# Paired-chunk loads, gated prefetch and a searched order in a sliding-window attention and two-MLP kernel

## The chip, the cores and the metric

One core of one Trainium2 chip runs the whole program. The metric is the device time of one execution in microseconds; of several runs the median is given.

## The reference

The inputs are queries, keys and values of 4 batches, 8 heads, 576 positions and 64 dimensions, and the weights of two MLPs. Everything is float32.

```python
scores = scale * q @ k.T                                  # per batch and head
scores = where(0 <= i - j < 128, scores - slope[h] * (i - j), -1e9)
attn = softmax(scores)                                    # + 1e-9 in the denominator
x = (attn @ v), heads side by side                        # 2304 tokens x 512
h = x @ w_in                                              # 2304 x 2048
x = (max(h, 0) + alpha * min(h, 0)) @ w_out               # 2304 x 512
h = max(x @ w1, x @ w2, x @ w3)                           # 2304 x 768
out = h @ w_out2                                          # 2304 x 512
```

The weights of both MLPs come as 64-bit floats, which the kernel turns into float32 itself.

## The kernel before, in words

The 2304 tokens are cut into nine chunks of 256 (c = 0 to 8). Attention works on one chunk and one pair of heads (hp = 0 to 3) at a time, so there are 36 such pairs of heads. `pair` (L710) does one: it loads queries and keys (L723), one transfer for each of the two heads, each into 64 partitions; it loads the values (L727, L751), scales the queries on POOL (L730), computes the scores on PE (L743), the softmax on DVE (L772), ACT (L778, L783) and POOL (L790), transposes on PE (L800) with copies on ACT (L808), the product with the values on PE (L820, L837, L844), and writes the result in two parts as input of the first MLP (L867 on ACT, L869 on DVE). In the first four chunks (`EARLY`) the loaded queries and keys lie in four buffers `w24` to `w27` that later hold weights; from the fifth chunk on they lie in a ring of two.

The first MLP runs through "items": a block of 128 hidden features for a chunk or two. An item's first product is L903 to L905 (`hidden_of`), the activation is L909 and L912 on DVE and L882 and L883 on ACT and DVE (tile `g`), and the second product is L931 (`products_of`). Each weight block is loaded as 64-bit words (`to_f32`, L411, tiles `w_b`, 512 KB each: `w0_b` is the first block of w_in, `w1_b` the first of w_out, and so on), split into words and rebuilt on ACT (L412, L414), DVE (L416 to L422) and POOL (L425), and split once more into two parts (`split`, L432 on ACT, L434 on DVE or POOL). A weight load is told to wait for the ACT instruction L414 of the weight four blocks earlier. Chunks 0 to 3 and all 32 weight blocks are worked on in the first 140 us. Beside and behind them come the rest of the first MLP (`pair_mlp`) and the second MLP (`second_mlp`: 18 steps of products L1057 and output products L1077, whose weights come back from DRAM by the loads at L1012).

No engine's order is written by hand. Every operation is recorded with an engine, a cost and a due time (`Plan.add`); `Plan.run` walks through all of them with these costs, and `Plan.issue` repeats that eight times (`ROUNDS`), each time with due times made from the walk before, and keeps the order whose planned end is earliest. The instructions are then put out in that order, engine by engine, and each engine executes its own in order, SP's transfers included.

Two kinds of matmuls have no use but to keep PE going: `keep_busy` in the attention of the first chunk (L366), and those that `Plan.keep_busy` puts in at L372 where PE's plan has room between 12 and 130 us:

```python
for _ in range(round((until - max(free, at) - FILL_LESS) / FILL_ONE)):
    self.idle(new())
```

Of the kernel before, what the change touches and what calls it, by code (L numbers as in the profile page):

```python
# [21 lines left out]
P = 128  # L22
# [64 lines left out]
class Plan:  # L87
# [90 lines left out]
    def issue(self):  # L178
        due, best = {op: op.due for op in self.ops}, None
        for _ in range(ROUNDS):  # L180
            start, end = self.run(due)
            whole = max(end.values())
            if not best or whole < best[0]:
                best = whole, start
            late = self.run({op: -t for op, t in end.items()}, back=True)[1]
            due = {op: -t for op, t in late.items()}

            users = {}
            for op in self.ops:
                for d in op.deps:  # L190
                    if d.eng == "sp":
                        users[d] = min(users.get(d, due[op]), due[op])
            due.update((d, t - DMA_LEAD) for d, t in users.items())
# [77 lines left out]


FILL_FROM, FILL_TO, FILL_LESS, FILL_ONE = 12.0, 130.0, 0.3, 0.215

KEEP = 3
ROUNDS = 8
DMA_LEAD = 3.0
# [13 lines left out]
def attention_then_two_mlps(ctx: ExitStack, tc: tile.TileContext, qkv, v, w_in, w_out, alpha, w123, w_out2, out):  # L291
# [59 lines left out]

    cq = const.tile([P, H // 2], F32, name="cq")
    for h in range(H):
# [52 lines left out]
    def to_f32(src, raw, wt, due, after, n=512):  # L406
# [3 lines left out]

        add("sp", 1.4 * n / 512, due - 24, lambda: nc.sync.dma_start(out=raw(), in_=src.bitcast(I32)), w=[raw], after=after)  # L411
        add("act", 0.05 + n / 966, due - 10, lambda: nc.scalar.activation(  # L412
# [294 lines left out]

    X, loads = {}, []

    def pair(k, j, hp, due):  # L710


        c = GROUPS[k][j]
        vv, z = v_r.new(), z_r.new()
        if c < EARLY:
            raw, pt = (w_s.new(2 * NF - 8 + 4 * i + (c * KD + hp) % 4, 2 + i) for i in range(2))
            ps = [p_r.new() for _ in range(2)]
        else:
            raw, pt, ps = qkv_r.new(), pt_r.new(), [p_r.new() for _ in range(2)]
        qs, heads = slice(N + P, 2 * N + P), range(2)  # L720
        for a in heads:
            rows = slice(a * D, (a + 1) * D)
            load = add("sp", 0.6, due - 16, lambda a=a, rows=rows: nc.sync.dma_start(  # L723
                out=raw()[rows, :10 * D], in_=qkv[2 * hp + a, c, rows, :10 * D]), w=[raw])
        if c == 0:
            loads.append(load)
        add("sp", 0.7, due - 9, lambda: nc.sync.dma_start(  # L727
            out=vv(), in_=v[hp, c].rearrange("p (k a d) -> p k a d", k=3, a=2)), w=[vv])

        add("pool", 0.45, due - 13, lambda: nc.gpsimd.tensor_scalar(  # L730
            out=raw()[:, qs], in0=raw()[:, qs], scalar1=cq[:, hp:hp + 1], scalar2=1.0, op0=ALU.mult, op1=ALU.mult),
            r=[raw], w=[raw])

        s = [early.new(1 + (2 * hp + a) % 3) if c == 0 else s_b.new() for a in heads]


        def scores():

            for n in range(2):
                for u in range(2):  # L740
                    for a in heads:
                        rows, b = slice(a * D, (a + 1) * D), 2 * u + n
                        nc.tensor.matmul(s[a]()[u * D:(u + 1) * D, n * R:(n + 1) * R],  # L743
                                         raw()[rows, qs.start + b * D:qs.start + (b + 1) * D],
                                         raw()[rows, b * D:b * D + R], start=True, stop=True)

        scored = yield dict(cost=0.9, due=due - 12, fn=scores, r=[raw], w=s)
        ve = ve_r.new() if c in MERGED else None
        if ve:
            for n in range(2):  # L750
                add("sp", 0.3, due - 9, lambda n=n: nc.sync.dma_start(  # L751
                    out=ve()[n * D:(n + 1) * D], in_=v[hp, c, (1 - n) * D:(2 - n) * D, n * P:(n + 2) * P].rearrange(
                        "p (k a d) -> p k a d", k=2, a=2)), w=[ve])
        if c == 0:
# [50 lines left out]
        else:  # L805
            add("pe", 0.58, due - 6, lambda: [transposes(a) for a in heads], r=ps, w=psts)
        for a in heads:
# [3 lines left out]
        if ve:  # L811
# [11 lines left out]

            at_q, handed = 2 * R, dict(cost=0.95, due=due - 3.5, fn=values, r=[pt, vv, ve])
            yield handed
            psv = handed["w"]
        else:
# [19 lines left out]

            yield dict(cost=1.1, due=due - 3.5, fn=values, r=[pt, vv, *(psv if at_q else [])], w=psv)
        if k >= PAIRED:
# [347 lines left out]
    def attend(i):  # L1197
# [3 lines left out]
        for turn, args in enumerate(list_i):  # L1201
# [7 lines left out]
            for pair_of in going[:1] if merged else list(going):  # L1209
# [8 lines left out]
                if late:  # L1218
                    first = x["fn"]
                    new.send(put(dict(cost=1.6, due=x["due"], fn=lambda first=first, scores=scores: (first(), scores["fn"]()),  # L1220
                                      r=x["r"] + scores["r"], w=x["w"])))
                else:
                    put(x)
# [81 lines left out]
```

## Time and profile before

| what | value |
| --- | --- |
| median of three runs | 787.7 us |
| the three runs | 786.4, 787.7, 790.71 us |
| the profiled execution's own time | 790.29 us |
| its span, first to last instruction | 788.4 us |
| PE busy | 767.3 us, 97% of the span |
| DVE, ACT, POOL busy | 570.6, 400.0, 359.6 us |
| mean granted clock of PE | 0.996 |

The span is what the rows of the trace are counted in, from its first instruction; the profiled execution took 1.9 us more than its span, and 2.6 us more than the median. A window gives the busy time of each engine in a stretch. A timeline row gives a start, a length, the engine, the line, the operation, the tiles (written <- read), the number of instructions, and in brackets the idle time ahead of them and what ended it. Matmul records can overlap, so the length of a group is longer than the distance to the next one.

### The profile page before, as it was taken

To read this page: it belongs to the slowest core of one execution; us is meant where nothing else is said; L and a number is where in the kernel's file an instruction comes from. 1 tells how busy PE (TensorE), PEld (TensorE's weight loads), DVE (VectorE), ACT (ScalarE), POOL (GpSimd) and SP (SyncE) were. 2 spreads that over 40 slices of the span, in tenths; PEclk is the share of its full clock that TensorE was granted. 3 is DMA by queue.
4 is the path that set the end of the run, shared out by engine and by line. 5 is a ranking of instruction groups with operands and counts; after the bars stand their busy time and mean duration, and the time that the engine had idled before them with its cause. 6 is when DMAs were issued, how large, how long until landed. Compare 5 with 4: busy or idle time off the path is not lost.

```text
span 788.4 us, 16787 instructions
## 1 busy us (share of the span) xinstructions
PE 767.3 (97%) x5881; PEld 662.5 (84%) x5887; DVE 570.6 (72%) x1382; ACT 400.0 (51%) x1113; POOL 359.6 (46%) x444
## 2 busy tenths in 40 slices
PE   7699999999999999999999999999999999999998
PEld 3478877778778788997888788899998999899996
DVE  5578898977665848999996879869983546734551
ACT  5789786756454555657674657444433102411101
POOL 5669656776655325555664432504353211702211
PEclk9989999999999999999999999999999999999999
DMA  8998355654674538356678967587795877555702
GB/s 223 246 332 269 96 167 169 203 178 146 216 254 150 178 118 298 124 168 197 206 236 255 332 197 279 204 305 261 268 357 196 271 243 252 186 188 199 227 1 80
DMA packets 85923, 167.04 MB, mean 212 GB/s; under 512 B 10576, under 2 KB 46800, under 8 KB 85840
## 3 DMA queue, kind: packets, MB, share of 16 engines
q1 hardware_dynamic: 85696, 165.98, 64.1%
q8 instruction: 46, 0.75, 0.4%
q14 instruction: 37, 0.30, 0.1%
q10 hardware_dynamic: 144, 0.01, 0.0%
HBM read 114.83 MB, written 51.12 MB: 210 GB/s over the span
## 4 chain that ended last, share of the span: by engine, by line
PE 52%; DVE 1%; ACT 0%; issue 0%; ACTq 0%
PE sb L1057 13%; PE hb L1057 12%; PE xb L615 5%; PE xb L1077 5%; PE sb L585 4%; PE hb L585 3%; PE hb L1077 3%; PE hb L615 3%; PE sb L615 3%; PE sb L1077 2%; DVE o L601 0%; DVE o L593 0%; DVE sb L593 0%; DVE g L606 0%; DVE v L419 0%
## 5 line engine op out<-in xcount | busy, mean ns | idle before, releaser
L931 PE MATMUL xb<-g,w_a 128*128 128x512 f32 (+1 forms) x624 | 127.3, 351 | 6.6 <-ACT g L882 5.8
L931 PEld LDWEIGHTS xb<-g,w_a 128*128 128x128 f32 x624 | 96.9, 191 | 24.8 <-ACT g L882 6.2
L790 POOL TENSOR_SCALAR p<-p,z 128x192 f32<-128x192 f32 x144 | 70.8, 506 | 67.7 <-DVE z L786 65.7
L425 POOL TENSOR_TENSOR v<-v,p 128x192 int32<-128x192 int32 (+1 forms) x72 | 45.8, 640 | 69.8 <-DVE v L422 23.5
L434 POOL TENSOR_TENSOR g<-p,g 128x384 fp32r<-128x384 f32 x18 | 20.9, 1161 | 116.5 <-ACT g L432 87.6
L903 PE MATMUL hb<-x_a,w_a 128*128 128x512 f32 (+1 forms) x208 | 73.2, 352 | 0.7 <-DVE x_a L869 0.7
L904 PE MATMUL hb<-x_a,w_a 128*128 128x512 f32 (+1 forms) x208 | 71.0, 341 | 0.0
L905 PE MATMUL hb<-x_a,w_a 128*128 128x512 f32 (+1 forms) x208 | 70.8, 340 | 0.0
L778 ACT ACTIVATE p<-p,z 128x192 f32<-128x192 f32 x144 | 64.4, 451 | 11.9 <-DVE z L772 11.5
L1057 PE MATMUL sb<-w_e,w_a 128*128 128x384 f32 x306 | 59.3, 334 | 0.0
L772 DVE CUSTOM_DVE_ANT_0 p<-sb,rel 128x192 f32<-128x192 f32 x128 | 39.5, 353 | 21.0 <-PE sb L743 15.1
L1057 PEld LDWEIGHTS sb<-w_e,w_a 128*128 128x128 f32 x306 | 53.8, 188 | 0.4
L425 POOL TENSOR_TENSOR wt<-wt,w_b 128x512 int32<-128x512 int32 x32 | 44.1, 1387 | 13.6 <-DVE wt L422 12.3
L615 PE MATMUL xb<-g,w_a 128*128 128x512 f32 x192 | 46.0, 389 | 0.0
L903 PEld LDWEIGHTS hb<-x_a,w_a 128*128 128x128 f32 x208 | 39.3, 189 | 7.4 <-issue 1.4
L1057 PE MATMUL hb<-w_e,x_a 128*128 128x384 f32 x234 | 45.4, 334 | 0.0
L1057 PE MATMUL hb<-w_e,w_a 128*128 128x384 f32 x234 | 45.4, 334 | 0.0
L434 POOL TENSOR_TENSOR w_a<-wt,w_a 128x512 fp32r<-128x512 f32 x25 | 34.9, 1394 | 22.2 <-ACT w_a L432 22.0
L905 PEld LDWEIGHTS hb<-x_a,w_a 128*128 128x128 f32 x208 | 39.4, 189 | 4.5
L1065 DVE TENSOR_TENSOR v<-hb,qkv 128x384 f32<-128x384 f32 x30 | 16.7, 555 | 36.6 <-PE hb L1057 36.6
L904 PEld LDWEIGHTS hb<-x_a,w_a 128*128 128x128 f32 x208 | 39.4, 189 | 4.4 <-DVE w_a L434 0.2
L432 ACT CAST w_a<-wt 128x512 fp32r<-128x512 f32 x57 | 35.0, 621 | 15.5 <-DVE wt L474 6.0
(223 smaller groups left out, 1951.0 us busy)
## 6 DMA issues: line engine op xcount, KB each, us to landing
w_a<-left SPq DMA_DIRECT2D x30, 512.0 KB, 5.2
x_a<-left SPq DMA_DIRECT2D x24, 512.0 KB, 5.3
w_b<-in_w_in SPq DMA_DIRECT2D x16, 512.0 KB, 5.7
w_b<-in_w_out SPq DMA_DIRECT2D x16, 512.0 KB, 6.2
left<-w_a SPq DMA_DIRECT2D x15, 512.0 KB, 5.6
v<-in_v SPq DMA_DIRECT2D x36, 192.0 KB, 3.2
p<-in_w SPq DMA_DIRECT2D x36, 192.0 KB, 3.2
qkv<-in_qkv SPq DMA_DIRECT2D x40, 160.0 KB, 3.0
```

The lines of the kernel that those rows point to most:

```text
L425: add("pool", n / 403, due - 5, lambda: nc.gpsimd.tensor_tensor(out=wt().bitcast(I32), in0=wt().bitcast(I32), in1=words(0), op=ALU.add), r ...
L434: add("pool" if pool_lo else "dve", n / 403 if pool_lo else 0.07 + n / 960, due + 1, lambda: eng.tensor_tensor(out=w()[:, 1, :n], in0=of() ...
L585: nc.tensor.matmul(to(), w()[:, a, ws], xs[k]()[:, b], start=(first and at_m == 0), stop=(last and at_m == 5), skip_group_check=True)
L615: nc.tensor.matmul(bs[m](), W_out[f]()[:, a, cols], g[f]()[:, b], start=(opens and f == fs[0] and not a and not b), stop=(closes and f == ...
L778: exps.append(add("act", 0.45, due - 10 + a, lambda i=i, n=n, p=p: nc.scalar.activation(out=part_of_p(p, n), in_=part_of_p(p, n), func=AF. ...
L790: z.readers.append(add("pool", 0.4, at_a + 0.2, lambda i=i, n=n, p=p: nc.gpsimd.tensor_scalar(out=part_of_p(p, n), in0=part_of_p(p, n), sc ...
L903: nc.tensor.matmul(to, wi()[:, 0, ws], x[:, 0, cols], start=(kk == 0), stop=False)
L904: nc.tensor.matmul(to, wi()[:, 1, ws], x[:, 0, cols], start=False, stop=False)
L905: nc.tensor.matmul(to, wi()[:, 0, ws], x[:, 1, cols], start=False, stop=(kk == KD - 1))
L931: nc.tensor.matmul(to, wo()[:, a, ms], g()[:, b, :n], start=(opens and not a and not b), stop=(closes and ends), skip_group_check=apart)
L1057: nc.tensor.matmul(to()[:, :TILE], Qs[q]()[:, a, ws], x[:, b], start=(first and n == 0), stop=(last and n == 5), skip_group_check=True)
L1077: nc.tensor.matmul(o(), g[j]()[:, a, b * P:(b + 1) * P], Wo[j]()[:, c], start=(j == 0 and not a and not c), stop=(j == NJ - 1 and a == 1), ...
```

## The change

Queries and keys of the first four chunks are loaded two chunks at a time: one transfer brings chunk c into partitions 0 to 63 and chunk c + 1 into partitions 64 to 127 of one buffer. For the even head of a pair of heads that is chunks 0 and 1, then 2 and 3; for the odd head chunk 0 alone (upper half, on ACT's queue), then 1 and 2, then 3 alone. The even head's data lie in `w24` to `w27`, the odd head's in `x10` to `x13`. The scale factor gets a column per head (`ch`); where only the upper half is loaded, DVE scales it, otherwise POOL. From the second chunk on every load of a pair of heads waits for the scores of the pair of heads four places back. The planner's costs for PE's attention work go up, those of some transfers go down. `Plan.issue` makes 40 trials: in each after the first the due times of the best one so far are blurred by random numbers, and four rounds start from there.

```diff
     def issue(self):
-        due, best = {op: op.due for op in self.ops}, None
-        for _ in range(ROUNDS):
-            start, end = self.run(due)
...
+        draw, best = random.Random(0), None
+        for trial in range(TRIALS):
+            if trial:
+                due = {op: t + draw.gauss(0.0, BLUR) for op, t in best[2].items()}
+            else:
+                due = {op: op.due for op in self.ops}
+            for _ in range(ROUNDS if trial else 2 * ROUNDS):
+                start, end = self.run(due)
...
+PREFETCH = 4
...
-ROUNDS = 8
+ROUNDS, TRIALS, BLUR = 4, 40, 1.5
...
-        add("sp", 1.4 * n / 512, due - 24, ...
+        add("sp", 1.35 * n / 512, due - 24, ...
...
+        qs, heads, ahead = slice(N + P, 2 * N + P), range(2), scored_ops[-PREFETCH:][:1] if c else []
         if c < EARLY:
-            raw, pt = (w_s.new(2 * NF - 8 + 4 * i + (c * KD + hp) % 4, 2 + i) for i in range(2))
+            pt, half = w_s.new(2 * NF - 4 + hp, 3), [(c + a) % 2 for a in heads]
+            for a in heads:
+                if c and half[a]:
+                    continue
+                first, last = (D if half[a] else 0), (D if c == EARLY - 1 else P)
+                KQ[hp, a] = raw = (qkv_r.new() if first == 0 and last == D else
+                                   w_s.new((2 * NF + KD * SETS[1] if a else 2 * NF - 8) + hp, 2))
+                part = slice(first, last)
+                r0 = (c - half[a]) * P + D
...
+                queue = nc.scalar if half[a] else nc.sync
+                load = add("sp", 0.82 if last - first == P else 0.6, due - 16, lambda ...:
+                           queue.dma_start(out=raw()[part, :10 * D], in_=from_[:, :10 * D]), w=[raw], after=ahead)
+                eng, e, cost = (nc.vector, "dve", 0.2) if half[a] else (nc.gpsimd, "pool", 0.45)
+                add(e, cost, due - 13, lambda ...: eng.tensor_scalar(
+                    out=raw()[part, qs], in0=raw()[part, qs], scalar1=ch[part, 2 * hp + a:2 * hp + a + 1], ...
...
-        scored = yield dict(cost=0.9, due=due - 12, fn=scores, r=[raw], w=s)
+        scored = yield dict(cost=1.0, due=due - 12, fn=scores, r=raws, w=banks)
+        scored_ops.append(scored)
```

Three places show how the order moves. The first is POOL's queue around the softmax of the fourth pair of heads (tile `z0_569`, now `z0_592`; L790, now L822, multiplies its four parts by the reciprocal sums), before and now.

```order
L730 TENSOR_SCALAR w24_c_418<-w24_c_418,cq_247 128x256
L730 TENSOR_SCALAR w25_c_452<-w25_c_452,cq_247 128x256
L790 TENSOR_SCALAR p0_568<-p0_568,z0_569 128x192
L790 TENSOR_SCALAR p0_576<-p0_576,z0_569 128x192
L790 TENSOR_SCALAR p0_568<-p0_568,z0_569 128x192
L790 TENSOR_SCALAR p0_576<-p0_576,z0_569 128x192
L425 TENSOR_TENSOR wt0_489<-wt0_489,w0_b_388 128x512
```

```order
L745 TENSOR_SCALAR x11_c_461<-x11_c_461,ch_248 128x256
L745 TENSOR_SCALAR x12_c_500<-x12_c_500,ch_248 128x256
L745 TENSOR_SCALAR x13_c_543<-x13_c_543,ch_248 128x256
L822 TENSOR_SCALAR p0_591<-p0_591,z0_592 128x192
L822 TENSOR_SCALAR p0_596<-p0_596,z0_592 128x192
L822 TENSOR_SCALAR p0_591<-p0_591,z0_592 128x192
L822 TENSOR_SCALAR p0_596<-p0_596,z0_592 128x192
L436 TENSOR_TENSOR wt0_564<-wt0_564,w1_b_412 128x512
```

The fourth pair's multiplications stood behind the scaling of the second pair of chunk 1 (`w25_c_452`); they now stand behind that of the odd heads of all four pairs of chunk 1, `x13_c_543` the last.

The second is SP's queue ahead of `w4_b`, the fifth weight block, before and now, with the semaphores that each transfer waits for (`DMAHW` is that of an earlier transfer, eight of them being used in turn; `PE`, `Pool` and `DVE` are the engines' own).

```order
L723 DMA qkv0_606<-in_qkv 64x640 [waits DMAHW5_49]
L723 DMA qkv0_606<-in_qkv 64x640 [waits DMAHW6_49]
L723 DMA qkv0_624<-in_qkv 64x640 [waits DMAHW7_49]
L723 DMA qkv0_624<-in_qkv 64x640 [waits DMAHW0_49]
L727 DMA v0_640<-in_v 128x384 [waits DMAHW1_49,PE_49]
L723 DMA w24_c_653<-in_qkv 64x640 [waits DMAHW2_49,PE_49,Pool_49]
L723 DMA w24_c_653<-in_qkv 64x640 [waits DMAHW3_49]
L411 DMA w4_b_666<-in_w_in 128x1024 [waits DMAHW4_49]
```

```order
L743 DMA x12_c_500<-in_qkv 128x640 [waits DMAHW2_49,DVE_49,PE_49]
L743 DMA x13_c_543<-in_qkv 128x640 [waits DMAHW3_49,DVE_49,PE_49]
L761 DMA v0_569<-in_v 128x384 [waits DMAHW4_49,PE_49]
L743 DMA w24_c_587<-in_qkv 128x640 [waits DMAHW5_49,PE_49,Pool_49]
L783 DMA ve0_600<-in_v 64x256 [waits DMAHW6_49]
L422 DMA w4_b_621<-in_w_in 128x1024 [waits DMAHW7_49]
L783 DMA ve0_600<-in_v 64x256 [waits DMAHW0_49]
L761 DMA v0_642<-in_v 128x384 [waits DMAHW1_49,PE_49]
L422 DMA w5_b_652<-in_w_out 128x1024 [waits DMAHW2_49]
```

The four loads of the fifth chunk (`qkv0_606`, `qkv0_624`) and one load of values are no longer ahead of `w4_b`: it was the 36th transfer of SP's queue and is now the 19th.

The third is ACT's queue around the first `g`, the activation of the MLP's first item (L882, now L914).

```order
L808 COPY w28_d_812<-sb0_781 128x384
L783 ACTIVATE z0_728<-z0_728 128x2 x2
L412 ACTIVATE wt0_817<-w4_b_666 128x512
L414 ACTIVATE w4_b_666<-w4_b_666 128x512
L412 ACTIVATE wt0_826<-w5_b_711 128x512
L882 CAST g0_844<-hb0_789 128x256
```

```order
L425 ACTIVATE w4_b_621<-w4_b_621 128x512
L840 COPY w28_d_830<-sb0_790 128x384
L840 COPY w28_d_830<-sb0_826 128x384
L914 CAST g0_834<-hb0_798 128x256
L815 ACTIVATE z0_733<-z0_733 128x2
L423 ACTIVATE wt0_853<-w4_b_621 128x512
L423 ACTIVATE wt0_857<-w5_b_652 128x512
```

Three steps on the weight blocks `w4_b` and `w5_b` stood ahead of the first `g`; one step on `w4_b` still does. Of the matmuls of the planner's own filling there were 45 and are now 28 (L372, now L383); those of the first chunk are 24 in both (L366, now L377).

## Rows read from the trace of the kernel before

**Rows 1.** The page: busy time by engine, and PE in 40 slices.
```profile
PE 767.3 (97%) x5881; PEld 662.5 (84%) x5887; DVE 570.6 (72%) x1382; ACT 400.0 (51%) x1113; POOL 359.6 (46%) x444
...
PE   7699999999999999999999999999999999999998
```

**Rows 2.** Windows: stretch, its length, then busy by engine, clock, DMA share, GB/s.
```profile
7.00:80.00 73.00, 63.28 (x800) 47.78 (x807) 50.92 (x189) 62.05 (x203) 51.36 (x73) 0.95 0.92 271
...
80.00:130.00 50.00, 49.93 (x576) 39.42 (x567) 44.30 (x120) 36.55 (x110) 31.61 (x38) 1.00 0.38 123
130.00:788.40 658.40, 652.30 (x4499) 574.36 (x4497) 473.59 (x1058) 300.12 (x800) 272.83 (x319) 1.00 0.64 212
```

**Rows 3.** Timeline of PE: start, length, work, and idle time before it.
```profile
5.17 1.56 PE L743 MATMUL xb<-w_c 64*64 64x192 f32 x16 [5.17 <-POOL w_c L730]
...
34.15 0.38 PE L372 MATMUL hb<-ident 128*128 128x512 bf16 x1
40.37 2.08 PE L931 MATMUL xb<-g,w_a 128*128 128x256 f32 x8 [5.84 <-ACT g L882]
```

**Rows 4.** Timeline of ACT, 0 to 62 us.
```profile
7.18 0.46 ACT L778 ACTIVATE p<-p,z 128x192 f32<-128x192 f32 x1 [4.76 <-DVE z L772]
...
35.93 0.66 ACT L412 ACTIVATE wt<-w_b 128x512 f32<-128x512 f32 x1 [3.19 <-DMA w_b<-in_w_in]
...
39.40 0.66 ACT L412 ACTIVATE wt<-w_b 128x512 f32<-128x512 f32 x1 [2.25 <-DMA w_b<-in_w_out]
39.96 0.36 ACT L882 CAST g<-hb 128x256 fp32r<-128x256 f32 x1
...
44.50 0.46 ACT L778 ACTIVATE p<-p,z 128x192 f32<-128x192 f32 x1 [1.21 <-DVE z L772]
```

**Rows 5.** Timeline of SP's transfers, and its waits in 10 to 60 us.
```profile
25.39 3.43 SPq L723 DMA_DIRECT2D qkv<-in_qkv  x4
28.92 0.53 SPq L727 DMA_DIRECT2D v<-in_v  x1
...
30.71 1.05 SPq L411 DMA_DIRECT2D w_b<-in_w_in  x2
...
SPq L727 <- PE hb L844: 4.3, 3, 3.5
```

**Rows 6.** Windows (columns as in rows 2): DMA at the start, stalled, and with weights.
```profile
2.00:25.00 23.00, 18.10 (x230) 10.81 (x234) 13.38 (x69) 15.93 (x63) 13.29 (x29) 1.00 1.00 240
25.00:29.00 4.00, 2.59 (x49) 1.75 (x41) 2.79 (x14) 4.00 (x16) 4.00 (x5) 1.00 0.54 148
...
41.00:45.00 4.00, 4.00 (x55) 2.97 (x54) 1.28 (x8) 2.55 (x6) 3.11 (x5) 0.60 1.03 405
```

**Rows 7.** Timeline of PE: the same five groups at two clocks end here.
```profile
45.60 0.39 PE L372 MATMUL sb<-ident 128*128 128x512 bf16 x1
...
50.61 0.88 PE L743 MATMUL sb<-w_c 64*64 64x192 f32 x16
...
54.16 0.49 PE L800 MATMUL sb<-ident,p 128*128 128x128 f32 x3
```

**Rows 8.** Groups by line, PE, 0 to 130 us: the planner's filling.
```profile
L372 PE MATMUL hb<-ident 128*128 128x512 bf16 x25 | 6.2, 379 | 0.1
...
L372 PE MATMUL sb<-ident 128*128 128x512 bf16 x16 | 4.1, 380 | 0.1
```

**Rows 9.** Tile w_c, 0 to 60 us: ns min/median/max of an issue on SP.
```profile
L723 SPq DMA_DIRECT2D w_c<-in_qkv x24: 465/472/1007, 0.7 to 52.1; - x24
```

**Rows 10.** Timeline of POOL (columns as in rows 3).
```profile
20.04 0.52 POOL L730 TENSOR_SCALAR w_c<-w_c,cq 128x256 f32<-128x256 f32 x1 [1.10 <-DMA w_c<-in_qkv]
21.45 2.58 POOL L790 TENSOR_SCALAR p<-p,z 128x192 f32<-128x192 f32 x4 [0.89 <-DVE z L786]
```

**Rows 11.** The second MLP: SP's waits (total, times, longest), one window.
```profile
SPq L1012 <- PE sb L1057: 51.3, 32, 7.9
...
580.00:590.00 10.00, 10.00 (x51) 8.84 (x50) 8.00 (x13) 4.85 (x10) 7.88 (x7) 1.00 1.02 382
```

More of the change, by code (lines that the diff above doesn't have):

```diff
@@ L178, in issue @@
     def issue(self):
-        due, best = {op: op.due for op in self.ops}, None
-        for _ in range(ROUNDS):
-            start, end = self.run(due)
[L182 to L193, printed above, removed]
+        draw, best = random.Random(0), None
[6 more added lines that the diff above has]
+                start, end = self.run(due)
+                whole = max(end.values())
+                if not best or whole < best[0]:
+                    best = whole, start, due
+                late = self.run({op: -t for op, t in end.items()}, back=True)[1]
+                due = {op: -t for op, t in late.items()}
+                users = {}
+                for op in self.ops:
+                    for d in op.deps:
+                        if d.eng == "sp":
+                            users[d] = min(users.get(d, due[op]), due[op])
+                due.update((d, t - DMA_LEAD) for d, t in users.items())
         free = 0.0
@@ L706, in pair_mlp @@
         return now
-    X, loads = {}, []
+    X, KQ, loads, scored_ops = {}, {}, [], []
     def pair(k, j, hp, due):
         c = GROUPS[k][j]
-        vv, z = v_r.new(), z_r.new()
+        vv, z, ps = v_r.new(), z_r.new(), [p_r.new() for _ in range(2)]
+        qs, heads, ahead = slice(N + P, 2 * N + P), range(2), scored_ops[-PREFETCH:][:1] if c else []
         if c < EARLY:
-            raw, pt = (w_s.new(2 * NF - 8 + 4 * i + (c * KD + hp) % 4, 2 + i) for i in range(2))
-            ps = [p_r.new() for _ in range(2)]
-        else:
[L719 to L724, printed above, removed]
+            pt, half = w_s.new(2 * NF - 4 + hp, 3), [(c + a) % 2 for a in heads]
[7 more added lines that the diff above has]
+                r0 = (c - half[a]) * P + D
+                from_ = (qkv[2 * hp + a].rearrange("c p x -> (c p) x")[max(r0, 0) + first:r0 + last] if half[a] == 0 else
+                         qkv[2 * hp + a, c, part])
+                queue = nc.scalar if half[a] else nc.sync
+                load = add("sp", 0.82 if last - first == P else 0.6, due - 16, lambda raw=raw, part=part, from_=from_, queue=queue:
+                           queue.dma_start(out=raw()[part, :10 * D], in_=from_[:, :10 * D]), w=[raw], after=ahead)
+                eng, e, cost = (nc.vector, "dve", 0.2) if half[a] else (nc.gpsimd, "pool", 0.45)
+                add(e, cost, due - 13, lambda raw=raw, part=part, eng=eng, a=a: eng.tensor_scalar(
+                    out=raw()[part, qs], in0=raw()[part, qs], scalar1=ch[part, 2 * hp + a:2 * hp + a + 1], scalar2=1.0,
+                    op0=ALU.mult, op1=ALU.mult), r=[raw], w=[raw])
+            raws = [KQ[hp, a] for a in heads]
+        else:
+            raw, pt, half = qkv_r.new(), pt_r.new(), heads
+            raws = [raw, raw]
+            for a in heads:
+                rows = slice(a * D, (a + 1) * D)
+                add("sp", 0.6, due - 16, lambda a=a, rows=rows: nc.sync.dma_start(
+                    out=raw()[rows, :10 * D], in_=qkv[2 * hp + a, c, rows, :10 * D]), w=[raw], after=ahead)
+            add("pool", 0.45, due - 13, lambda: nc.gpsimd.tensor_scalar(
+                out=raw()[:, qs], in0=raw()[:, qs], scalar1=cq[:, hp:hp + 1], scalar2=1.0, op0=ALU.mult, op1=ALU.mult),
+                r=[raw], w=[raw])
@@ L725, in pair @@
         if c == 0:
             loads.append(load)
[L727 to L734, printed above, removed]
+        add("sp", 0.55, due - 9, lambda: nc.sync.dma_start(
+            out=vv(), in_=v[hp, c].rearrange("p (k a d) -> p k a d", k=3, a=2)), w=[vv], after=ahead)
@@ L737, in scores @@
+        banks = [early.new(1 + (2 * hp + a) % 3) if c == 0 else s_b.new() for a in heads]
+        s = [banks[i] for i in half]
         def scores():
@@ L805, in pair @@
         else:
-            add("pe", 0.58, due - 6, lambda: [transposes(a) for a in heads], r=ps, w=psts)
+            add("pe", 0.65, due - 6, lambda: [transposes(a) for a in heads], r=ps, w=psts)
         for a in heads:
@@ L1219, in attend @@
                     first = x["fn"]
-                    new.send(put(dict(cost=1.6, due=x["due"], fn=lambda first=first, scores=scores: (first(), scores["fn"]()),
+                    new.send(put(dict(cost=1.95, due=x["due"], fn=lambda first=first, scores=scores: (first(), scores["fn"]()),
                                       r=x["r"] + scores["r"], w=x["w"])))
```

19 lines of the change are left out of this document (11 added, 8 removed).

## The prediction
> **What bounds the kernel now.** The page comes first: PE is busy for 767.3 of 788.4 us, and of its 40 slices only the first two and the last are below nine tenths [rows 1]. The windows say what that is worth: from 130 us on PE is busy for 652.3 of 658.4 us, and what is missing there, 6.1 us, contains the copies and stores behind the last matmul; from 80 to 130 us it lacks 0.07 us [rows 2]. No change to loads, order or waits takes anything from a full PE, so a gain has to come from the first 80 us, and it is carried to the end one for one. In that stretch ACT is the engine beside PE: from 7 to 80 us it works 62.05 of 73 us, more than DVE (50.92) and POOL (51.36) [rows 2].
>
> Next the timeline of PE. Its one long stop lies at 34.5 us: 5.84 us idle until ACT hands over the first `g` [rows 3]. The timeline of ACT says why the `g` was late: ACT executes in order, and ahead of L882 stand three steps on weight blocks (the third place of the order). For the first it waited 3.19 us, for the third 2.25 us, both times for a transfer of a weight block [rows 4]. Without those 5.44 us the `g` would have been there at about 34.5, when PE stopped.
>
> The timeline of SP says why the blocks were late. The first of them was issued at 30.71 [rows 5], as the 36th transfer of that queue. Ahead of it went four loads for the fifth chunk at 25.39 and a load of values at 28.92, which had waited 3.5 us for a product of the fourth pair of heads [rows 5]. Meanwhile the DMA engines, full from 2 to 25 us at 240 GB/s, were half empty from 25 to 29 us [rows 6]. So both the queue's order and its rate delay `w4_b`. The rate is told by two windows with full DMA engines: 240 GB/s while queries and keys go into 64 partitions among other loads, 405 GB/s from 41 to 45 us with little else than weight blocks, into 128 [rows 6].
>
> **The change, part by part.** All terms are changes within the profiled execution of 790.29 us; it lies 2.6 us above the median of 787.7, and I take them off the median.
>
> *The order on SP.* `w4_b` is the 19th transfer of SP instead of the 36th. With what ACT's queue now carries, 6912 KB (7.08 MB) instead of 7296 KB go ahead of it or with it: 2880 KB in nine transfers of 320, 640 in four of 160, 768 in four of 192, 64, and 2560 of weights. Counted from 2 us, this lands at 2 + 7.08/0.240 = 31.5 us at the lower rate and at 2 + 7.08/0.405 = 19.5 us at the upper one. ACT, whose work ahead of that step is about the same, gets there at 35.93 - 3.19 = 32.7 us, so it is in time at either rate; `w5_b` has moved behind the `g` altogether. The stop of PE goes: **-5.84 us**.
>
> *The clock.* After the stop PE's granted clock is at the lower of its two levels, 1.2 instead of 2.4 GHz, for most of 41 to 45 us (mean 0.60) [rows 6]. Five groups (twelve matmuls of L931, the scores and the values of a pair of heads) take from 40.37 [rows 3] to 45.60 there, 5.23 us, and from 50.61 to 54.16, 3.55 us, at the full clock [rows 7]. With the stop goes the difference: **-1.7 us**.
>
> *Filling.* 45 matmuls without use become 28. The 41 recorded took 6.2 + 4.1 = 10.3 us [rows 8], 0.25 us each, so 17 are at most 4.3 us. They stand where the plan has room, so most of that would be idle time instead; in part they are fewer because the plan now counts more time for PE's own work. Between -4.3 and 0 I take 0.
>
> *The loads themselves.* Twelve transfers of queries and keys fall away (32 become 20), and four go to ACT: 16 issues of 0.47 us [rows 9], 7.5 us of SP's time, which only counts where SP issues without waiting. On ACT the four cost some 1.9 us in its 4.76 us of idle time ahead of the first exponential [rows 4]. POOL scales 16 times as before; DVE's four scalings and eight small memsets lie ahead of work it waits for. The first scores start at 5.17 after the first load and its scaling [rows 3]. The first pair now needs 480 KB, with 320 KB of the second pair beside it, in place of 320: at 240 GB/s at most 2 us later, at 405 GB/s and from two queues at once about as early. Taken: 0, since PE, DVE and ACT have idle time in the first chunk to make up for it (ACT keeps 73 - 62.05 - 5.44 = 5.5 us of it) [rows 2].
>
> *The gate.* Loads that wait for the scores four pairs back wait for little that their buffers did not already make them wait for; what it changes is which loads stand ahead of a weight block, and that is counted above.
>
> *The rest of the order.* It moves blocks of matmuls up to the end. The trace shows 6.1 us of idle time there [rows 2]; a better order can take no more than that, a worse one might double it: between -6.1 and +6.1. I take 0, nearest to the 0.07 us of 80 to 130 us, where a full PE hides whatever the order does.
>
> Sum: -5.84 - 1.7 = -7.5, so 787.7 - 7.5 = **780.2 us**. ACT agrees: of its 10.95 us of idle time from 7 to 80 us [rows 2] the two waits and the 1.21 us that follow from the slow PE [rows 4] are 6.65.
>
> *Rule and trace.* Rows 6 show 240 GB/s and 405 GB/s with the DMA engines equally full. The Trainium skill (SBUF — State Buffer, Door 1: The DMA port swizzle) says that partitions 0 to 63 reach only half of the ports by which DMA writes SBUF, and measures 196 against 328 GB/s for transfers of 1 MiB. Rows 6 agree in the ratio, 0.59 against its 0.60. By that rule the merged loads run at the upper rate and the first rival below falls away. By the rows alone the lower rate stays open, and that rival keeps a chance.
>
> **The rivals.**
>
> *The rate does not rise* (packets, not partitions, set the 240 GB/s). Then POOL stops: the fourth pair's multiplications stand behind the scaling of `x13_c`, and with it 5824 KB (5.96 MB) have gone: at 240 GB/s it lands at 2 + 24.8 = 26.8 us. Before, these multiplications began at 21.45 [rows 10]. They come 5.9 us later with the scaling, the first item of the MLP needs them, and of the 7.5 us some 1.6 remain: **786.1 us**. It decides below 5.96 MB / 19.45 us = 306 GB/s. For it speaks that all kinds of loads lie mixed in that window; against it the 405 GB/s.
>
> *The search pays.* Half of the filling's bound and half of the late idle time are won: -7.5 - 2.1 - 3 = -12.6, **775.1 us**. Against it: ACT's idle time, of which only 4.3 us are left after the sum.
>
> *The late order costs more than the start gives (slower).* The place is the second MLP. Its weights come back by L1012, whose buffers come free when PE has read them; SP waits for PE there 32 times, up to 7.9 us [rows 11], the DMA engines are full in a window like 580 to 590 us [rows 11], and the order of the products in its 18 steps is changed. If each step now stops PE for 0.7 us, that is 12.6 us: 787.7 - 7.5 + 12.6 = **792.8 us**. It decides from 11.4 us of new idle time, 0.63 us a step. For it: the order is chosen by planned time alone, which leaves no slack on purpose. Against it: the window of 658 us shows PE as good as full under an order that was chosen the same way.
>
> *The gate does nothing, and something else holds the first `g`* (another wait takes the stop's place, `w6_b` behind a load of values): half of the stop stays, 784 us.
>
> **How the numbers follow.** Forecast (779 to 783): 0.58. Rate does not rise: 0.14. Search pays: 0.10. Slower late: 0.10. Another wait: 0.08. Half a per cent, 3.9 us, is about what a measurement of this kernel tells from no change. Faster by more: 0.58 + 0.10 and 0.05 of the last and of the first rival's better part, 0.73. Within: 0.17. Slower: 0.10. The range runs from 775 us, the search's case, to 787 us, the first rival's with the half width of its runs; it leaves out the slower case and the tails.
>
> **What would show it.** Right: no idle time of PE over 2 us between 10 and 80 us, clock at 1.00 throughout; the first `g` at 33 to 35 us; ACT's waits for weight blocks gone; DMA above 300 GB/s from 2 to 20 us; `w4_b` issued before 22 us; PE's idle time behind 130 us within 3 us of 6.1. Wrong: POOL waiting for `x13_c` beyond 22 us (first rival), PE waiting at L1057 (now L1089) for weights, or a `g` that ACT has ready and PE does not yet want.

## The result and the profile after

The changed kernel takes **780.73 us** (median of 5 runs, 779.02 to 781.75) against 787.7 us before (5 runs): the ratio is **0.990** with a 95% interval of 0.9879 to 0.9921 (the quotient of the two medians is 0.991). The forecast was 780.2 us, between 775 and 787.

The profiled execution took 780.38 us, its span is 778.6. The page answers to [rows 1]:

```profile
PE 763.7 (98%) x5864; PEld 660.9 (85%) x5870; DVE 577.2 (74%) x1394; ACT 397.7 (51%) x1113; POOL 360.9 (46%) x444
...
PE   7999999999999999999999999999999999999998
```

PE is idle for 778.6 - 763.7 = 14.9 us instead of 21.1, and its second slice is full. The windows (stretch, length, busy by engine, granted clock, DMA share, GB/s) answer to [rows 2, 6]:

```profile
2.00:20.00 18.00, 14.53 (x157) 7.96 (x159) 10.74 (x53) 11.85 (x43) 10.93 (x24) 1.00 1.02 351
7.00:80.00 73.00, 69.74 (x905) 53.26 (x906) 61.76 (x226) 68.88 (x232) 60.61 (x79) 1.00 0.80 272
25.00:29.00 4.00, 3.01 (x47) 2.01 (x42) 3.88 (x15) 4.00 (x15) 3.80 (x5) 1.00 0.95 322
80.00:130.00 50.00, 50.00 (x524) 39.83 (x522) 46.35 (x119) 37.81 (x108) 35.20 (x41) 1.00 0.53 174
130.00:778.60 648.60, 642.04 (x4430) 566.70 (x4428) 466.88 (x1026) 289.76 (x774) 261.08 (x310) 1.00 0.63 211
```

From 2 to 20 us the DMA engines move 351 GB/s; the kernel before moved 247 in the same stretch, both with the engines full. From 25 to 29 us they stay full. The clock is 1.00 in every window. The last row is the one to compare: from 130 us on PE is as full as before, so its busy time there is the work that was still left at 130 us, as long as the clock stays at 1.00 there. It is 642.04 instead of 652.30 us, 10.26 us less, while the idle time in it went from 6.1 to 6.56. Up to 130 us PE is idle for 130 - (763.7 - 642.04) = 8.3 us instead of 15.0. The gain is all made in the first 130 us, and carried to the end.

Four timelines show how (start, length, work, idle time before it and what ended it). ACT [rows 4]:

```profile
8.37 0.46 ACT L810 ACTIVATE p<-p,z 128x192 f32<-128x192 f32 x1 [2.65 <-DVE z L804]
...
33.02 0.39 ACT L914 CAST g<-hb 128x256 fp32r<-128x256 f32 x1
```

SP, with the issue of `w4_b` [rows 5]:

```profile
18.30 1.28 SPq L422 DMA_DIRECT2D w_b<-in_w_in  x1
```

POOL, with the scalings that end with `x13_c` and the fourth pair's multiplications [rows 10]:

```profile
20.43 1.54 POOL L745 TENSOR_SCALAR x_c<-x_c,ch 128x256 f32<-128x256 f32 x3
22.85 2.30 POOL L822 TENSOR_SCALAR p<-p,z 128x192 f32<-128x192 f32 x4 [0.88 <-DVE z L818]
```

PE [rows 3]:

```profile
4.70 0.90 PE L774 MATMUL xb<-w_c 64*64 64x192 f32 x2 [4.70 <-POOL w_c L745]
5.97 0.58 PE L774 MATMUL xb<-x_c 64*64 64x192 f32 x1 [0.38 <-DVE x_c L745]
26.96 1.06 PE L869 MATMUL hb<-w_d,v 128*64 128x64 f32 x16 [0.58 <-ACT w_d L840]
```

`w4_b` is issued at 18.30 instead of 30.71; ACT waits for no weight block any more and writes the first `g` at 33.02 instead of 39.96, nothing idle before it. The 0.58 us at 26.96 is PE's longest wait from 10 to 80 us. POOL does the fourth pair at 22.85, 1.4 us later than before, with no transfer to wait for.

The filling [rows 8] takes 7.0 us in 24 records of its 28 matmuls, instead of 10.3 in 41 of 45 (groups by line, 0 to 130 us):

```profile
L383 PE MATMUL hb<-ident 128*128 128x512 bf16 x16 | 4.6, 380 | 0.2
L383 PE MATMUL sb<-ident 128*128 128x512 bf16 x8 | 2.4, 381 | 0.3 <-DVE z L804 0.2
```

The stop (5.84), the slow clock (1.7) and 3.3 us of filling are 10.8 us, against 10.26 us of work done earlier. So the profile would credit filling too, which the sum took at 0. But the profiled execution of before lay 2.6 us above its median: the spans differ by 9.8 us, the medians by 7.0. In the sets of runs behind the experiments the kernel before had medians of 789.2 to 790.4 us, near that profiled time, and the changed kernel run beside it was 8.2 us faster. Only runs that change one thing can say which term is real.

### The profile page after: what moved, and what is told of

Same layout as the page of the kernel before. It is cut to its first block, busy times and chain, and to the rows that moved or that the text cites. A ratio compares the mean times of both kernels' runs of the same rounds, so it can differ in the third digit from the quotient of the medians.

```text
span 778.6 us, 16737 instructions
## 1 busy us (share of the span) xinstructions
PE 763.7 (98%) x5864; PEld 660.9 (85%) x5870; DVE 577.2 (74%) x1394; ACT 397.7 (51%) x1113; POOL 360.9 (46%) x444
## 4 chain that ended last, share of the span: by engine, by line
PE 57%; DVE 2%; DMA 1%; issue 1%; ACT 1%; POOL 0%; SPq 0%; POOLq 0%; ACTq 0%; DVEq 0%
PE sb L1089 13%; PE hb L1089 12%; PE xb L626 6%; PE xb L1109 5%; PE sb L596 4%; PE hb L596 4%; PE hb L1109 3%; PE hb L626 3%; PE sb L626 3%; PE sb L1109 2%; PE xb L963 1%; DVE v L427 1%; DMA p<-in_w 1%; PE hb L937 0%; PE hb L936 0%
## 5 line engine op out<-in xcount | busy, mean ns | idle before, releaser
L963 PE MATMUL xb<-g,w_a 128*128 128x512 f32 (+1 forms) x624 | 125.1, 347 | 2.4 <-ACT g L914 2.4
L822 POOL TENSOR_SCALAR p<-p,z 128x192 f32<-128x192 f32 x144 | 75.8, 541 | 62.5 <-DVE z L818 55.7
L436 POOL TENSOR_TENSOR v<-v,p 128x192 int32<-128x192 int32 (+1 forms) x72 | 43.6, 608 | 79.6 <-DVE v L433 40.4
L810 ACT ACTIVATE p<-p,z 128x192 f32<-128x192 f32 x144 | 64.3, 451 | 10.2 <-DVE z L804 9.9
L445 POOL TENSOR_TENSOR w_e<-p,w_e 128x384 fp32r<-128x384 f32 x21 | 23.0, 1099 | 62.3 <-ACT w_e L443 62.3
L935 PEld LDWEIGHTS hb<-x_a,w_a 128*128 128x128 f32 x208 | 39.4, 189 | 7.5 <-issue 2.2
L941 DVE TENSOR_SCALAR t<-hb,alpha_sb 128x512 f32<-128x512 f32 (+1 forms) x52 | 32.3, 622 | 17.0 <-PE hb L937 16.6
L937 PEld LDWEIGHTS hb<-x_a,w_a 128*128 128x128 f32 x208 | 39.4, 189 | 4.6
```

The costliest lines, as they stand in the source:

```text
L436: add("pool", n / 403, due - 5, lambda: nc.gpsimd.tensor_tensor(out=wt().bitcast(I32), in0=wt().bitcast(I32), in1=words(0), op=ALU.add), r ...
L445: add("pool" if pool_lo else "dve", n / 403 if pool_lo else 0.07 + n / 960, due + 1, lambda: eng.tensor_tensor(out=w()[:, 1, :n], in0=of() ...
L810: exps.append(add("act", 0.45, due - 10 + a, lambda i=i, n=n, p=p: nc.scalar.activation(out=part_of_p(p, n), in_=part_of_p(p, n), func=AF. ...
L822: z.readers.append(add("pool", 0.4, at_a + 0.2, lambda i=i, n=n, p=p: nc.gpsimd.tensor_scalar(out=part_of_p(p, n), in0=part_of_p(p, n), sc ...
L935: nc.tensor.matmul(to, wi()[:, 0, ws], x[:, 0, cols], start=(kk == 0), stop=False)
L937: nc.tensor.matmul(to, wi()[:, 0, ws], x[:, 1, cols], start=False, stop=(kk == KD - 1))
```

## The experiments

Three theories. **1**: the early weight blocks and the rate of the merged loads make the gain. **2**: the searched order makes it. **3**: what matters in the loads is their number, not their partitions. Ratios are to the kernel before in the same set of runs (787.7 us in the first set, 789.2 to 790.4 us in the others), with 95% intervals. The "first `g`" is the start, in us, of the MLP's first activation on ACT; "left" is PE's busy time from 130 us to the end, "PE idle" its idle time in the whole span, "filling" the busy time of the planner's own matmuls up to 130 us, all in us and from one profiled execution each.

| kernel | ratio | interval | GB/s, 2 to 20 us | first `g` | left | PE idle | filling |
| --- | --- | --- | --- | --- | --- | --- | --- |
| before | 1 | | 247 | 39.96 | 652.30 | 21.1 | 10.3 |
| changed | 0.9900 | 0.9879 to 0.9921 | 351 | 33.02 | 642.04 | 14.9 | 7.0 |
| changed, again | 0.9892 | 0.9868 to 0.9916 | 335 | 33.18 | 644.40 | 17.0 | 7.3 |
| two halves | 0.9924 | 0.9905 to 0.9944 | 273 | 36.85 | 647.76 | 17.1 | 7.3 |
| two columns | 0.9892 | 0.9867 to 0.9916 | 327 | 33.71 | 643.14 | 14.5 | 7.3 |
| no gate | 0.9898 | 0.9882 to 0.9914 | 331 | 35.09 | 645.58 | 17.3 | 5.5 |
| no search | 0.9933 | 0.9920 to 0.9947 | 347 | 33.92 | 645.18 | 20.8 | 3.0 |
| other seed | 0.9925 | 0.9906 to 0.9945 | 325 | 34.94 | 644.80 | 18.1 | 6.3 |
| old costs | 0.9960 | 0.9947 to 0.9972 | 342 | 35.10 | 647.91 | 15.8 | 10.6 |
| no filling | 0.9877 | 0.9856 to 0.9898 | 343 | 33.52 | 642.60 | 18.5 | 0 |
| search alone | 0.9989 | 0.9977 to 1.0001 | 266 | 37.73 | 651.51 | 20.0 | 8.1 |
| gate alone | 0.9952 | 0.9933 to 0.9971 | 251 | 33.79 | 648.16 | 15.2 | 10.0 |
| merge alone | 0.9945 | 0.9925 to 0.9965 | 316 | 35.07 | 647.55 | 16.6 | 10.2 |
| all but merge | 0.9951 | 0.9935 to 0.9967 | 269 | 36.42 | 648.40 | 17.6 | 7.5 |

Two of these profiles hold a stop of PE of over 2 us behind 130 us: the changed kernel's second one (2.33 us, until DVE ends it at 357.69; this execution took 784.91 us, the median is 781.42) and that of two halves (2.12 us, until ACT ends it at 315.80; the slowest of its six executions). Windows around them: the changed kernel's first profile, its second, two halves.

```profile
350.00:370.00 20.00, 18.97 (x84) 15.39 (x83) 18.94 (x33) 15.84 (x37) 13.13 (x14) 1.00 0.49 154
```

```profile
350.00:370.00 20.00, 17.68 (x71) 14.17 (x70) 15.11 (x29) 13.69 (x31) 10.29 (x11) 0.91 0.44 141
```

```profile
310.00:330.00 20.00, 17.76 (x125) 16.97 (x124) 18.25 (x50) 12.24 (x37) 11.58 (x14) 0.91 0.50 156
```

A clock of 0.91 for 20 us is up to 1.8 us, so that much of "left" in these two rows is slow clock and not work. The same program shows it in one execution and not in another, so differences of "left" below 2 us are not read here. And in every kernel for which the planner was run anew, which is all but two halves, two columns, no filling and the changed kernel itself, the order of everything has changed along with the part that is named.

### Two halves, two columns: partitions or number

Both keep the changed kernel's order on every engine. The first issues each merged transfer as two of 64 partitions:

```diff
...
-  queue.dma_start(out=raw()[part, :10 * D], in_=from_[:, :10 * D])
+  [queue.dma_start(out=raw()[part.start + i:part.start + i + D, :10 * D], in_=from_[i:i + D, :10 * D])
+   for i in range(0, part.stop - part.start, D)]
...
```

> The changed kernel with the same order on every engine, but each merged transfer of queries and keys issued as two transfers into 64 partitions (chunk c, then chunk c + 1): the same bytes into the same buffers. Theory 1 (the first 64 or 128 partitions set the rate): 2 to 20 us falls from 351 GB/s to between 240 and 300, the multiplications of the fourth pair on POOL start later than their 22.85 us by 2 to 5 us, the first g comes as much later than 33.0 us, and the time is 783 to 786 us. Theory 2 (the searched order gives the gain): the order is the same, so 780 to 782 us. Theory 3 (the number of transfers counts, since only eight are in flight): as theory 1 here, told apart by the run with two column halves.

The second also makes two transfers of it, each of 128 partitions and half of the columns:

```diff
...
+  [queue.dma_start(out=raw()[part, i * D:(i + 5) * D], in_=from_[:, i * D:(i + 5) * D])
+   for i in range(0, 10, 5) if part.stop - part.start == P] or
   queue.dma_start(out=raw()[part, :10 * D], in_=from_[:, :10 * D])
...
```

> The changed kernel with the same order on every engine, but each merged transfer into 128 partitions issued as two transfers of 128 partitions and half the columns (1280-byte rows): as many transfers as with two halves of 64 partitions. Theory 1 (partitions set the rate): 2 to 20 us stays above 320 GB/s, first g within 1 us of 33.0, time 780 to 782 us. Theory 3 (the number of transfers counts): as the run with two halves of 64 partitions, 783 to 786 us. Theory 2 (the order): 780 to 782 us.

One window of each, columns as above, two halves first:

```profile
2.00:20.00 18.00, 13.24 (x140) 7.47 (x141) 9.46 (x51) 10.56 (x40) 9.34 (x23) 1.00 1.05 273
```

```profile
2.00:20.00 18.00, 14.63 (x143) 7.50 (x143) 10.07 (x53) 11.13 (x41) 9.90 (x23) 1.00 1.04 327
```

The same bytes, the same number of transfers, the DMA engines full in both: 273 against 327 GB/s. What differs is the partitions that one transfer reaches; the shorter rows of the half columns cost little beside it (327 against 335 to 351). The Trainium skill (DMA: Bandwidth & Descriptors, Rules for kernel authors) advises one transfer of 128 partitions in place of two to the halves, since these share the same DMA engines and so serialize. The advice agrees with 273 against 351; its reason does not cover the 327, since the two column transfers share the engines as well. The half of the ports, which the Trainium skill (SBUF — State Buffer, Door 1: The DMA port swizzle) gives to 64 partitions, covers both in direction; the ratio of 273 to 327 is 0.83, in a window where other loads lie among these.

With two halves the first rival's mechanism stands on POOL's timeline, and behind it on PE's:

```profile
25.96 0.54 POOL L746 TENSOR_SCALAR x_c<-x_c,ch 128x256 f32<-128x256 f32 x1 [3.77 <-DMA x_c<-in_qkv]
...
27.79 1.62 POOL L823 TENSOR_SCALAR p<-p,z 128x192 f32<-128x192 f32 x4
```

```profile
28.27 0.33 PE L833 MATMUL hb<-ident,p 128*128 128x128 f32 x1 [1.75 <-POOL p L823]
```

POOL waits 3.77 us for a scaled load, the fourth pair comes at 27.79 instead of 22.85, and the first `g` at 36.85. By the ratios this costs 0.24 to 0.32%, 1.9 to 2.5 us; by the medians of two halves and two columns, 784.75 and 781.45 us, it is 3.3 us. The intervals overlap, so the size is loose, but it is less than the 5.9 us that the rival gave it: the multiplications came 4.9 us later, and PE waited 1.75 us for them. Part of the cost is the clock, in windows of two halves:

```profile
24.00:28.00 4.00, 2.13 (x48) 1.58 (x48) 3.23 (x14) 3.83 (x14) 1.49 (x3) 1.00 1.06 245
28.00:32.00 4.00, 3.10 (x26) 2.27 (x26) 1.73 (x11) 2.08 (x6) 4.00 (x7) 0.64 1.03 338
32.00:36.00 4.00, 4.00 (x40) 3.14 (x40) 3.00 (x8) 3.99 (x15) 4.00 (x5) 0.93 1.05 278
```

PE was busy for 2.13 of 4 us, and then the granted clock was 0.64 and 0.93: at most 4 x 0.36 + 4 x 0.07 = 1.7 us.

### One part alone, one part left out

Gate alone adds the waits for the scores four pairs back to the kernel before; merge alone has the merged loads with neither gate, search nor new costs; search alone and all but merge go by their names.

```diff
+    ahead = scored_ops[-PREFETCH:][:1] if c else []
...
-                out=raw()[rows, :10 * D], in_=qkv[2 * hp + a, c, rows, :10 * D]), w=[raw])
+                out=raw()[rows, :10 * D], in_=qkv[2 * hp + a, c, rows, :10 * D]), w=[raw], after=ahead)
...
```

> The kernel before with the gate alone (from the second chunk on, loads of a pair of heads wait for the scores four pairs back); loads into 64 partitions, costs and eight rounds as before. The plan puts w4_b at place 26 of SP's queue instead of 36, the loads of the fifth chunk behind it. Theory 1: the stop shrinks to under 3 us though the rate stays near 240 GB/s, 3 to 6 us less than before. If the rate is what matters: the stop stays, 0 to 2 us less than before.

> The merged loads alone: no gate, old costs, eight rounds. w4_b is the 24th transfer of SP. Theory 1: 2 to 20 us above 320 GB/s, the stop under 2 us, first g at 33 to 36 us, 4 to 7 us less than before. Theory 2 (the search gives most): 0 to 3 us less than before.

> The kernel before with 40 trials and nothing else: loads, waits and costs as before; w4_b stays the 36th transfer of SP. Theory 1 (the stop ahead of the first g goes because weight blocks come early): the stop stays, over 3 us, with PE's clock at its lower level behind it, and the time is 0 to 3 us less than before. Theory 2 (the searched order gives most): 4 to 7 us less than before.

> Gate, new costs and search, but the loads of the first four chunks into 64 partitions as before: the change without its first part. w4_b is the 26th transfer. Theory 1 with the rate as a second cause: 2 to 20 us stays under 290 GB/s, first g at 34 to 38 us, 3 to 6 us less than before, so the merged loads are worth 2 to 5 us of the change. If order and gate do all of it: 7 to 9 us less than before.

Search alone keeps the stop. PE's timeline, then ACT's:

```profile
38.14 1.73 PE L937 MATMUL xb<-g,w_a 128*128 128x256 f32 x8 [3.98 <-ACT g L888]
```

```profile
34.55 0.67 ACT L420 ACTIVATE w_b<-w_b 128x512 int32<-128x512 uint32 x1 [2.06 <-DMA w_b<-in_w_in]
37.17 0.66 ACT L418 ACTIVATE wt<-w_b 128x512 f32<-128x512 f32 x1 [1.40 <-DMA w_b<-in_w_out]
37.73 0.36 ACT L888 CAST g<-hb 128x256 fp32r<-128x256 f32 x1
```

The two waits of [rows 4] are there, shorter (2.06 and 1.40 us), and so is the stop of [rows 3]; the ratio's interval holds 1. Gate alone ends the stop at the old rate of 251 GB/s, by the order on SP. SP's timeline, then ACT's:

```profile
21.07 0.58 SPq L411 DMA_DIRECT2D w_b<-in_w_in  x1
```

```profile
33.79 0.38 ACT L885 CAST g<-hb 128x256 fp32r<-128x256 f32 x1
```

So the order alone removes the stop. Merge alone removes it too, at 316 GB/s (above 320 was expected), but there `w4_b` is the 24th transfer, not the 36th, and is issued 8 us earlier than before:

```profile
22.62 0.33 SPq L422 DMA_DIRECT2D w_b<-in_w_in  x1
```

The order has moved along with the rate, and that the rate alone would do it is not shown. Each of the two gives about half a per cent (0.9952, 0.9945). Gate, merged loads and new costs together, with no search, give 0.67% (below) and not the sum of both; that the stop can be removed only once fits this. All but merge shows what the loads into 64 partitions leave, on PE's timeline, with a window behind it:

```profile
24.77 0.33 PE L809 MATMUL hb<-ident,p 128*128 128x128 f32 x1 [1.81 <-POOL p L799]
26.77 1.33 PE L809 MATMUL hb<-ident,p 128*128 128x128 f32 x5 [1.68 <-POOL p L799]
```

```profile
25.00:29.00 4.00, 2.32 (x18) 1.73 (x21) 0.26 (x1) 1.52 (x7) 3.56 (x6) 0.58 1.06 255
```

Two waits for POOL's multiplications, and a clock of 0.58 from 25 to 29 us. Its time is that of the gate alone.

The gate taken out of the changed kernel, the search being made anew:

```diff
-  qs, heads, ahead = slice(N + P, 2 * N + P), range(2), scored_ops[-PREFETCH:][:1] if c else []
+  qs, heads, ahead = slice(N + P, 2 * N + P), range(2), []
```

> The changed kernel without the gate: loads of a pair of heads wait for their buffers alone. The planner, run anew, puts w4_b at place 24 of SP's queue. Theory 1: w4_b is issued later than 18.3 us but still before 28 us, so the first g comes between 33 and 36 us and the time is 781 to 784 us. A rival, that the gate alone gives the gain: a stop of 4 us and more ahead of the first g, 785 to 788 us.

The ratio is 0.9898 against 0.9900: beside merged loads and a searched order the gate is worth nothing that can be measured, as far as one searched order of each tells.

### The search, and its seed

```diff
-ROUNDS, TRIALS, BLUR = 4, 40, 1.5
+ROUNDS, TRIALS, BLUR = 4, 1, 1.5
```

> The changed kernel with one trial of eight rounds in place of 40 trials; loads, gate and costs stay. w4_b is the 18th transfer of SP instead of the 19th. Theory 1 (early weight blocks give the gain): the stop ahead of the first g stays away (no idle time of PE over 2 us from 10 to 80 us), 780 to 783 us. Theory 2 (the search gives it): 785 to 788 us.

```diff
-        draw, best = random.Random(0), None
+        draw, best = random.Random(1), None
```

> Another seed of the random numbers that blur the due times in the search; all else as in the changed kernel. If the gain is that of the early weight blocks and the merged loads (the prediction), any order that keeps them gives 0.988 to 0.993, no stop of PE above 2 us from 10 to 80 us, and 350 GB/s. If the searched order itself carries the gain of some 2.6 us over the kernel without a search, it comes back with another seed, within 1 us; if that was the luck of one draw, this one lies up to 3 us above, near the 0.9933 without a search.

Without the search the gain is 0.67% instead of 1.0%. The 785.2 us lie in the range expected for the second theory, while the sign of the first holds: no stop over 2 us. With another seed the gain is 0.75% (at 325 GB/s, not the expected 350): the intervals of these two overlap almost wholly. So the third of a per cent between them and the changed kernel belongs to one draw, not to searching as such; how often a draw pays, two seeds don't tell. Part of the loss without the search is seen in two windows:

```profile
28.00:32.00 4.00, 3.06 (x35) 2.85 (x32) 3.20 (x8) 3.91 (x15) 2.65 (x4) 0.69 0.78 244
32.00:36.00 4.00, 4.00 (x60) 3.06 (x59) 2.42 (x7) 2.82 (x7) 2.49 (x4) 0.88 0.25 101
```

The clock fell, after PE had been busy for 2.81 and 2.67 of 4 us in the two stretches before. 0.69 and 0.88 in 4 us each are at most 4 x 0.31 + 4 x 0.12 = 1.7 us of work lost, out of 645.18 - 642.04 = 3.1 more work left at 130 us. With the other seed the clock is 1.00; there PE waits, the two longest times for the copy into the MLP's input on DVE (L901):

```profile
22.85 0.84 PE L832 MATMUL hb<-ident,p 128*128 128x128 f32 x6 [1.40 <-DVE x_a L901]
26.87 0.87 PE L832 MATMUL hb<-ident,p 128*128 128x128 f32 x6 [0.60 <-DVE x_a L901]
```

### Filling and costs

The 28 matmuls of the filling left out, the order of all else kept:

```diff
-FILL_FROM, FILL_TO, FILL_LESS, FILL_ONE = 12.0, 130.0, 0.3, 0.215
+FILL_FROM, FILL_TO, FILL_LESS, FILL_ONE = 12.0, 12.0, 0.3, 0.215
```

> The 28 matmuls of the planner's filling left out, the order of everything else kept. 24 of them were recorded, 7.0 us of PE's time. If they stand where PE would be idle, as the prediction took it (0 of a bound of 4.3 us), the time stays within 0.2% of the changed kernel, PE's idle time grows by some 7 us and its busy time falls by as much. If they cost what they last, it is 7 us or 0.9% faster (0.981 of the kernel before). If the clock needs them, the granted clock falls below 1.00 somewhere between 12 and 130 us and the time grows, by 2 us or more.

The old costs under merged loads, gate and search; of seven, the one of the scores:

```diff
-        scored = yield dict(cost=1.0, due=due - 12, fn=scores, r=raws, w=banks)
+        scored = yield dict(cost=0.9, due=due - 12, fn=scores, r=raws, w=banks)
```

> The planner's costs of the kernel before with merged loads, gate and search of the changed one. If the costs matter for nothing but the number of fillings (the prediction), the time is that of the changed kernel within 0.3%, with some ten more fillings. If the higher costs of PE's attention work are what keeps the first 80 us free of stops, PE waits for more than 1 us at several places between 10 and 80 us and the time is 0.992 to 0.995 of the kernel before.

And the changed kernel itself beside them:

> The changed kernel as it is, once more, so that the three others of this set can be compared with it on one chip. 0.990 of the kernel before, within 0.2%: some 780 to 782 us, DMA above 330 GB/s from 2 to 20 us, first g at 33 to 34 us, some 15 us of idle time of PE in all.

Without filling, windows as above:

```profile
7.00:80.00 73.00, 65.33 (x878) 50.30 (x874) 61.54 (x225) 68.30 (x230) 59.99 (x79) 1.00 0.81 270
...
130.00:778.30 648.30, 642.60 (x4435) 567.26 (x4433) 467.13 (x1028) 290.69 (x777) 260.58 (x310) 1.00 0.64 212
```

PE's busy time of the whole span falls from 763.7 to 759.8, its idle time grows from 14.9 to 18.5, the work left at 130 us stays (642.60), and the clock stays at 1.00. Some 7 us had been expected for both: the lengths of the records, 7.0 us, overstate what the filling takes from PE. The intervals of 0.9877 and 0.9892 overlap. The 28 matmuls stand where PE would have been idle, and keep nothing up that the clock needed here. Whether the version without them is better by a tenth of a per cent these runs don't tell.

With the old costs the time is longer. The filling, groups by line, and the last window:

```profile
L383 PE MATMUL sb<-ident 128*128 128x512 bf16 x22 | 5.8, 380 | 0.9 <-DVE z L804 0.9
L383 PE MATMUL hb<-ident 128*128 128x512 bf16 x19 | 4.8, 380 | 0.0
```

```profile
130.00:783.80 653.80, 647.91 (x4465) 570.48 (x4463) 471.01 (x1043) 295.45 (x792) 266.81 (x316) 1.00 0.64 212
```

41 records again, 10.6 us, and PE is idle for 15.8 us, hardly more than the 14.9 of the changed kernel. 5.9 us more is left at 130 us, and the time is 786.78 against 781.42 us. Neither expectation came: it is outside 0.3%, but PE's longest wait from 10 to 80 us is 0.96 us. Up to 130 us PE spends 9.9 us idle and 10.6 on filling, 20.5 us without useful work, against 8.3 + 7.0 = 15.3 in the changed kernel; these 5.2 us are the loss. That the filling is its cause is not shown. PE's timeline shows both kinds: ahead of nine of these matmuls PE waits 0.89 us for DVE, and behind four others PE has to wait all the same:

```profile
29.56 2.13 PE L383 MATMUL sb<-ident 128*128 128x512 bf16 x9 [0.89 <-DVE z L804]
...
38.66 1.04 PE L383 MATMUL sb<-ident 128*128 128x512 bf16 x4
40.32 0.39 PE L935 MATMUL hb<-x_a,w_a 128*128 128x256 f32 x1 [0.62 <-DVE x_a L901]
```

Behind the nine the next product starts at once, so it may have been ready before; behind the four it was not. And merge alone, with the old costs and 10.2 us of filling, is about as fast as no search, with the new costs and 3.0 us (0.9945 and 0.9933). What is slower is the order that these costs gave, in this draw of the search; costs, filling and draw were not separated.

## Why the prediction was right, and where only its sum was

**The order on SP (-5.84) and the clock (-1.7): the mechanism right, the size not settled.** Each sign that it named is there: `w4_b` before 22 us (18.30), the first `g` between 33 and 35 (33.02), ACT's waits for weight blocks gone, no idle time of PE over 2 us, clock 1.00. In the changed kernel's profile PE's idle time up to 130 us falls by 6.6 us, from 15.0 to 8.3, as much as the stop lasted and a little more. The runs that remove the stop with one part, gate alone and merge alone, win 4.1 and 4.9 us of the 7.5. Their clock is at 1.00, but PE's idle time up to 130 us falls by only 3.8 and 3.1 us, to 11.2 and 11.9: the stop is gone, and PE waits elsewhere, in merge alone 1.25 us for DVE and 1.40 for POOL. Their orders are new throughout, so whether the terms were too large or these orders lose again what the stop gave is open.

**Filling (0): right for the 28 that are left** (no filling: the same time). For the 17 that went no run isolates a cost.

**The rest of the order (0): the term that was mis-sized.** The draw of the search is worth some 2.6 us (785.2 us without it, 0.9933 against 0.9900; 784.19 against 781.42 us with another seed), inside the bounds of 6.1 but not the 0 that was taken. Most of it lies in the first 130 us, where 3.1 us more is left without the search and 2.8 with the other seed, and not in the late idle time, where the bound was read: that is 6.56 us in the changed kernel, 7.6 and 7.2 in these two, 6.1 before. The old costs lose more, 5.4 us, again in the first 130 us.

So 780.2 against 780.73 us is closer than the sum can claim, and the closeness is in part luck: an order put at 0 moves the time by 2.6 us from one seed to the next, and the gain was 7.0 us in one set of runs and 8.2 in another. Either the stop and the clock gave their 7.5 us in this order, or they gave 4 to 5 and the order the rest; the parts were measured beside others or without them and don't say which.

**The loads (0) and the rate: right.** 351 GB/s against the threshold of 306 of the first rival, the first scores at 4.70 instead of 5.17. By the Trainium skill's rule on the ports (SBUF — State Buffer, Door 1: The DMA port swizzle) that rival fell away; the trace agrees in direction, with 273 against 327 GB/s at one and the same order.

**The gate (0): right beside the merged loads** (0.9898 without it). Alone it gives about half of what the whole change gives (0.9952), through the order on SP.

**The rivals.** The rate that does not rise was run as two halves: its mechanism appears where it was put, at a cost of 2 to 3 us instead of 5.9. The search's 775.1 us did not come: search alone is worth nothing that can be measured (0.9989), and what one draw gave beside the other parts came for the most part from the first 130 us, not from the late idle time. The second MLP, the slower case, did not come: 6.56 us idle behind 130 us, where it needed 11.4 us more than before. Another wait for the first `g` did not come: nothing idle ahead of it.

## What to carry to other kernels

Where a stop comes from a load that stands behind other loads, look at the queue's order and at the rate together, and test each alone: the order removed it at an unchanged rate, and a second remedy has only the rest to win. A rate at full DMA engines depends on the transfers' shapes: here two transfers of 64 partitions were worth merging into one of 128. And when a planner inserts filler or picks among orders by its own costs, its costs and its random draw are part of the change: measure more than one draw, and read how much useful work is left at a point behind which the bottleneck is full and the clock does not fall, for that counts filler, stops and slow clock ahead of it in one number.

## What was not expected

Full DMA engines say nothing of the rate: at a share of 1.02 to 1.05 they moved 273 GB/s with loads into 64 partitions, 327 and 351 with loads into 128. And the clock did not need the filling. Windows without filling, then with the other seed:

```profile
28.00:32.00 4.00, 2.73 (x45) 2.52 (x46) 3.52 (x15) 4.00 (x15) 3.79 (x6) 1.00 0.78 246
```

```profile
28.00:32.00 4.00, 3.78 (x49) 2.88 (x49) 3.30 (x16) 4.00 (x18) 4.00 (x7) 1.00 0.74 210
```

Without filling the clock is 1.00 in this stretch, after PE had been busy for 3.50 and 3.05 of 4 us in the two stretches before. In the kernel without a search it was 0.69 there, a mean of its two levels, after 2.81 and 2.67 of 4 us; with the other seed it was 1.00 after 2.29 and 2.92. What made it fall in the one and not in the other is not shown by these rows.
